# Fused attention and two MLPs: attention in chunks of 11 or 12 blocks instead of 12 and 9, score heads dealt out evenly, x rows at another offset

## The chip, the cores and the metric

The kernel runs on one core of one Trainium2 chip. The metric is the device time of one execution in microseconds. A core has TensorE (PE; its weight loads are shown as PEld), VectorE (DVE), ScalarE (ACT), GpSimd (POOL) and SyncE (SP); in this kernel SP and ACT issue the DMA transfers.

## The reference

Attention over 4 batches, 12 heads, 448 rows and 64 columns, with one 12 x 12 matrix that mixes heads before the softmax and one that mixes them after it. Its output, 1792 rows of 768, goes through two MLPs.

```python
scores = scale * np.matmul(q, k.transpose(0, 1, 3, 2))
scores = np.einsum('bhij,hg->bgij', scores, w_pre)
scores = scores - np.max(scores, axis=-1, keepdims=True)
attn = np.exp(scores)
attn = attn / (np.sum(attn, axis=-1, keepdims=True) + 1e-09)
attn = np.einsum('bhij,hg->bgij', attn, w_post)
attn_out = np.matmul(attn, v)
# x = attn_out as 1792 x 768
x = ((x @ w1) * (x @ w2) @ w3) @ w_out        # first MLP, w1 and w2 768x1024
out = np.maximum(x @ w_in, 0.0) ** 2 @ w_out2  # second MLP, d_ff 2048
```

## The kernel before

All operands are float32; most matmuls split an operand into a high and a low part and add three products (`mm3`). The program has three parts on one core: the product of w3 and w_out (`Prod34`, up to some 125 us), attention, and the MLPs (`Moe`), of which the first matmuls are issued while attention ends.

**Chunks and blocks.** The 448 query rows of a batch are cut into four chunks (`CHUNKS`: first row, rows, blocks), 120, 120, 120 and 88 rows. A chunk is cut into blocks of at most 10 rows, 12, 12, 12 and 9 of them, 45 per batch and 180 in all. `first[n]` is the number of the first block of chunk n, n from 0 to 15. A block holds 10 rows times 12 heads, so that one matmul with a 120 x 120 matrix mixes the heads.

**Score heads.** For a chunk and a head, `scores` does two matmuls (high and low part of q) into one of three PSUM buffers `sc`; `evac` copies it on ACT to the tile `s0` or `s1` (even and odd chunks), which keeps a chunk's 12 heads. The chunk after next uses the same tile again.

**A step.** `attention_step(A, d, ev)` issues step d: two blocks, 2d and 2d+1. `regroup` (SP, L378) brings the blocks 2d+4 and 2d+5 from `s` into the layout with heads on partitions (`r`, six buffers). On TensorE follow `premix` (L386), this step's score heads (L364), `tmix` of the blocks of two steps ago (L442), and `pv`, when it is planned. ACT does, in this order, the exponentials (`expo`), the evacuations of score heads, `p_hi`, its share of `p2` and `pv_out`; DVE does `rowmax`, `p_lo`, the reciprocals, `p2`, and the casts of q and k; POOL does a small addition and the low parts of q and k. The lists `ORDER`, `NEEDS` and `LAG` set this. `pv` multiplies a finished chunk by v, in two halves of 48 TensorE instructions; `pv_out` copies the half and stores it to `xd`.

**The plan.** `attention_plan` puts into every step which heads, loads and casts belong to it. It counts in blocks and halves the number (`ev.setdefault(step // 2, ...)`). The 12 heads of chunk n are spread over the block numbers in which chunk n-1 is on its way:

```python
for t, h in spread(first[n - 1] - RG + AT["sc"], first[n] - RG - 1, range(NH)):
    add(t, "scores", n, h)
```

with `RG` = 4 and `AT["sc"]` = 1. Loads of q are issued 6 block numbers ahead of the first of their four heads, the casts 4 ahead; k's six pairs come every 4 block numbers.

**The end of attention.** In step `closed` = (first[15] - RG) // 2 the tiles of the scores are given up and `Moe`'s pool `wp` takes their place. From there `tail_plan` issues, by block number, the loads of the first quarter's x rows (`load_x`), their split into parts (`split_x`, ACT and POOL), and the loads, joins (three DVE operations each) and splits of the first weights. After the last `pv` come the matmuls `e`, `early` ones of the first MLP; then `begin` loads the second quarter's x rows, and `run` goes through all other units of the MLPs. `new_xy` allocates x rows with some spare columns ahead and behind.

Of the kernel before, what the change touches and what calls it, by code (L numbers as in the profile page):

```python
# [17 lines left out]
B, NH, S, D = 4, 12, 448, 64  # L18
DM, FF1, FF2 = 768, 1024, 2048
NT = B * S  # L20
IC = 120
CHUNKS = [(0, 120, 12), (120, 120, 12), (240, 120, 12), (360, 88, 9)]
JC, JP = 4, 112
TB = 448
HT = 896
# [10 lines left out]
def fused_kernel(ctx, tc, q, k, v, w_pre, w_post, w1, w2, w3t, wo, win, wo2, eye, out):  # L36
# [3 lines left out]
    def pool(stack, name, side="left", space=None):  # L40
        kw = {"space": space} if space is not None else {}
        return stack.enter_context(tc.tile_pool(name=name, bufs=1, side=side, reuse_waits="tile", **kw))
# [5 lines left out]
    def f32(ap):  # L48
        return ap.bitcast(F)
# [179 lines left out]
    for n in range(16):  # L229
        _, ic, nr = CHUNKS[n % 4]  # L230
        o = 0
# [4 lines left out]
    first = {}  # L236
# [4 lines left out]
    RG = 4  # L241

    class Attention:
# [84 lines left out]
        def load_q(self, n, g4):  # L328
            b, c = divmod(n, 4)
            i0, ic, _ = CHUNKS[c]  # L330
            o = 12 * i0 + 4 * g4 * ic
            raw = self.ka.tile([128, 4 * IC], F, tag="qraw", name=f"qraw{n}_{g4}", bufs=2)
            nc.sync.dma_start(raw[:, : 4 * ic], q[b, :, o : o + 4 * ic])
            self.qraw[n, g4] = raw[:, : 4 * ic]

        def high_q(self, n, g4):
            th = self.ka.tile([128, 4 * IC], R, tag="qh", name=f"qh{n}_{g4}", bufs=3)
            th = self.qh[n, g4] = th[:, : 4 * CHUNKS[n % 4][1]]
            if n:
                nc.vector.tensor_copy(th, self.qraw[n, g4])  # L340
            else:
                nc.scalar.activation(th, self.qraw[n, g4], AF.Copy)

        def low_q(self, n, g4):
            tl = self.ka.tile([128, 4 * IC], R, tag="ql", name=f"ql{n}_{g4}", bufs=3)
            tl = self.ql[n, g4] = tl[:, : 4 * CHUNKS[n % 4][1]]
            nc.gpsimd.tensor_tensor(tl, self.qraw.pop((n, g4)), f32(self.qh[n, g4]), ALU.subtract)
# [5 lines left out]
        def scores(self, n, h):  # L353
            b, c = divmod(n, 4)
            ic = CHUNKS[c][1]
            assert ("k", b, h // 2) in self.done
            if h == 0:
                self.st[n] = (self.ka if n % 2 == 0 else self.kc).tile(
                    [IC, NH, S], F, tag=f"s{n % 2}", name=f"s{n}"
                )  # L360
            sc = self.ps.tile([IC, S], F, tag="sc", name=f"sc{n}_{h}", bufs=3)
            g4, hh = divmod(h, 4)
# [6 lines left out]
        def evac(self, n, h):  # L369
            ic = CHUNKS[n % 4][1]  # L370
            nc.scalar.activation(self.st[n][:ic, h], self.sc.pop((n, h))[:ic], AF.Copy)  # L371
            self.done.add(("s", n, h))
# [75 lines left out]
        def p2_evac(self, g, eng):  # L448
            n, r, nr, o, cnt = blocks[g]
            if n not in self.p2:  # L450
                self.p2[n] = self.kb.tile([JP, JC, NH, IC], F, tag="p2", name=f"p2{n}", bufs=2)
            d = self.p2[n][:, :, :, o : o + cnt].rearrange("p j g i -> p (j g) i")
# [40 lines left out]
            eng = nc.sync if n < 15 else nc.scalar  # L493
            eng.dma_start(xd[n // 4, :, 3 * y : 3 * y + 3, o : o + ic], u[:, :, :ic])

    def spread(lo, hi, items):
        return [(lo + i * (hi - lo) // len(items), x) for i, x in enumerate(items)]


    AT = {"sc": 1, "lq": 6, "hq": 4, "pv": 5, "k": -11, "ks": 4, "v": -6}  # L500


    TAIL = {"w": 5, "ws": 2, "w8": 13, "n": 4, "x": -1, "xs": 2, "xn": 4, "xt": 2, "h": 7, "hn": 1}

# [7 lines left out]
    def attention_plan():  # L512
        ev = {}

        def add(step, kind, *a):
            ev.setdefault(step // 2, {}).setdefault(kind, []).append(a)

        for n in range(16):
            b = n // 4
            if n:  # L520
                for t, h in spread(first[n - 1] - RG + AT["sc"], first[n] - RG - 1, range(NH)):
                    add(t, "scores", n, h)
                    if h % 4 == 0:
                        add(t - AT["lq"], "load_q", n, h // 4)
                        add(t - AT["hq"], "high_q", n, h // 4)
            for y in range(2):
                add(first[n + 1] + AT["pv"] + (5 if n < 15 else 0) * y, "pv", n, y)
        for b in range(1, B):
            for r in range(NH // 2):
                t = first[4 * b - 2] + AT["k"] + AT["ks"] * r  # L530
                add(t - 3, "load_k", b, r)
                add(t, "high_k", b, r)
        for b in range(B):
            add(first[4 * b] + AT["v"] if b else -10, "load_v", b)
        return ev


# [45 lines left out]
    class Moe:  # L583
# [95 lines left out]
        def new_xy(self, name, t):  # L679
            p = self.ap if t else self.wp  # L680
            out = []

            for e, before, after in (("h", 24, 0), ("l", 16, 24)):
                if t:
                    before = after = 0
                x = p.tile([128, before + 6 * TB + after], R, tag=f"xy{e}{t}", name=f"{name}{e}{t}")
                out.append(x[:, before : before + 6 * TB].rearrange("p (c n) -> p c n", n=TB))
            return tuple(out)
# [113 lines left out]
    with tc.manual_schedule(), ExitStack() as base:  # L802
        const = pool(base, "const")
        sa, sb, s34, stg, sps = ExitStack(), ExitStack(), ExitStack(), ExitStack(), ExitStack()
        ka = pool(sa, "ka")
        P = Prod34(pool(s34, "p34"), pool(stg, "stg", "right"), ka)
        A = Attention(const, ka, None)
        A.setup_load()
        ev = attention_plan()
        step = iter(range(-5, (first[16] + AT["pv"]) // 2 + 2))  # L810

        def prologue(i):
            def at(kind):
                return [x for x, t in enumerate(PRO[kind]) if t == i]

            if i == PRO["pre"]:
                A.setup_pre()
            for kind in ("load_k", "load_q"):
                for x in at(kind):
                    getattr(A, kind)(0, x)  # L820
            for x in at("evac"):
                if PRO["scores"][x] < i:
                    A.evac(0, 2 * x)
                    A.evac(0, 2 * x + 1)
            for kind in ("low_k", "high_k", "split_q"):
                for x in at(kind):
                    getattr(A, kind)(0, x)
            for x in at("scores"):
                for h in (2 * x, 2 * x + 1):
                    A.scores(0, h)  # L830
                    if PRO["evac"][x] == i:
                        A.evac(0, h)
            if i == PRO["post"]:
                A.setup_post()
            if i == 15:
                stg.close()
                A.kc = pool(sb, "kc", "right")
            if i >= 15:
                for _ in range(PRO["steps"][i - 15]):
                    attention_step(A, next(step), ev)  # L840

        with ExitStack() as s8:
            ps8 = pool(s8, "ps8", space=PSUM)

            P.half0(ps8, prologue)
        A.ps = ps = pool(sps, "ps", space=PSUM)
        tags = iter(("tp", "tp", "pv", "sp", "tp", "tp", "pv", "tp"))

        def space(m):
            tag = next(tags)  # L850
            return ps.tile([128, HC], F, tag=tag, name=f"q34_{m}", bufs=1 if tag == "pv" else 2)

        P.half1(space, lambda i: prologue(8 + i))
        s34.close()
        A.kb = pool(sb, "kb", "right")
        closed = (first[15] - RG) // 2
        M, tail = None, {}
        for d in step:
            attention_step(A, d, ev)
            if d == closed:  # L860
                sa.close()
                M = Moe(pool(sa, "wp"))
                tail = M.tail_plan()
                heads = (x for i in range(2) for x in M.early(
                    i, lambda i: ps.tile([128, TB], F, tag="sc", name=f"e{i}", bufs=3)
                ))
            for g in (2 * d, 2 * d + 1):
                for a in tail.pop(g - 2 * closed - 1, []):
                    a()
                for _ in range(TAIL["hn"] if g >= nb + TAIL["h"] else 0):  # L870
                    next(heads, None)
        for u in sorted(tail):
            for a in tail[u]:
                a()
        for _ in heads:
            pass
        sb.close()
        sm = ExitStack()
        M.begin(pool(sm, "ap", "right"))
        sps.close()  # L880
        M.run(pool(sm, "psm", space=PSUM))
        sm.close()
        sa.close()
# [51 lines left out]
```

## Time and profile before

| | us |
|---|---|
| median of three runs | 1378.08 (1377.71 to 1380.04) |
| the profiled execution | 1376.75 |
| its span, first to last instruction | 1374.9 |
| TensorE busy in it | 1322.3 |
| DVE, ACT, POOL busy in it | 920.9, 708.7, 414.7 |

The profile is of one execution. Its times count from the first instruction. A matmul's end is modelled, so the distance between the starts of two matmuls says more than the length of one. The granted clock of TensorE is given as a share of 2.4 GHz; 0.5 is the lower level, 1.2 GHz, and a value between is a mean over a stretch.

### The profile page before, as it was taken

The page shows a single profiled execution, that of the slowest core. Times are in us where ns is not written, and L with a number is a line of the kernel's source. Part 1 is how long each engine was busy: PE and PEld are TensorE (multiplying, and loading weights), DVE is VectorE, ACT ScalarE, POOL GpSimd, SP SyncE. Part 2 cuts the span into 40 slices and gives each one's busy share as a digit, 9 for nine tenths or more (in the row PEclk, how much of TensorE's full clock was granted, in tenths as well). Part 3 has the DMA queues.
Part 4 walks back from the last instruction along what each step waited for, and adds up shares of the span by engine and source line. Part 5 has one row for each costly group of instructions (what it writes and reads, how often), then busy time and mean ns, then how long its engine had stood idle before and what let it go on. Part 6 is the DMA issues. An engine that isn't in the chain of part 4 may idle for free.

```text
span 1374.9 us, 23972 instructions
## 1 busy us (share of the span) xinstructions
PE 1322.3 (96%) x8858; PEld 1149.9 (84%) x8858; DVE 920.9 (67%) x1555; ACT 708.7 (52%) x1529; POOL 414.7 (30%) x432
## 2 busy tenths in 40 slices
PE   5789999999999997899999999999999999999998
PEld 5687767767767775899999999999999999999998
DVE  8975977887887788555217953986555228945972
ACT  4456877777877876343224533443334224533430
POOL 4541432341342113222222322233222222322231
PEclk9889999999999999999999999999999999999999
DMA  7774445545554435433123432355443123432441
GB/s 213 224 237 139 157 157 171 188 147 179 166 186 148 140 101 161 140 113 113 55 66 104 126 127 81 112 183 178 126 116 96 54 81 103 131 116 81 126 146 58
DMA packets 95513, 183.76 MB, mean 134 GB/s; under 512 B 20581, under 2 KB 62053, under 8 KB 94949
## 3 DMA queue, kind: packets, MB, share of 16 engines
q1 hardware_dynamic: 89861, 178.82, 41.5%
q10 hardware_dynamic: 5536, 3.42, 0.8%
q8 instruction: 70, 1.15, 0.3%
q14 instruction: 46, 0.38, 0.1%
HBM read 129.52 MB, written 14.16 MB: 104 GB/s over the span
## 4 chain that ended last, share of the span: by engine, by line
PE 82%; DVE 5%; ACT 4%; issue 4%; DMA 2%; POOL 1%; SPq 0%; ACTq 0%; DVEq 0%; POOLq 0%
PE l L55 50%; PE y L55 8%; PE sp L386 7%; PE tp L442 6%; PE pv L483 5%; PE sc L364 4%; ACT p L400 1%; PE q L55 1%; DVE f L94 1%; DVE f L96 1%; DMA r<-s 1%; DVE f L98 1%; ACT ph L425 1%; ACT s L371 1%; DVE p L457 1%
## 5 line engine op out<-in xcount | busy, mean ns | idle before, releaser
L116 POOL TENSOR_TENSOR wl<-f,wh 128x384 fp32r<-128x384 f32 (+1 forms) x176 | 195.9, 1117 | 498.2 <-ACT wh L112 483.1
L94 DVE TENSOR_SCALAR f<-y 128x384 int32<-128x384 int32 (+2 forms) x209 | 154.3, 738 | 88.1 <-POOL wl L116 81.3
L386 PE MATMUL sp<-r,kpre 120*120 120x448 f32 x360 | 157.0, 558 | 2.6 <-DMA r<-s 1.4
L400 ACT ACTIVATE p<-sp,nm 120x448 f32<-120x448 f32 x180 | 113.2, 636 | 74.8 <-DVE nm L392 73.1
L392 DVE TENSOR_REDUCE nm<-sp 120x1 f32<-120x448 f32 x180 | 108.4, 620 | 62.5 <-PE sp L386 56.0
L98 DVE SCALAR_TENSOR_TENSOR f<-raw,f 128x384 int32<-128x384 int32 (+2 forms) x209 | 139.6, 668 | 6.2
L96 DVE SCALAR_TENSOR_TENSOR f<-y,f 128x384 int32<-128x384 int32 (+2 forms) x209 | 135.9, 650 | 6.2
L112 ACT ACTIVATE wh<-f 128x384 fp32r<-128x384 f32 (+1 forms) x176 | 96.6, 549 | 83.8 <-DVE f L98 83.2
L55 PE MATMUL l<-blh,wh 128*128 128x448 f32 x384 | 139.4, 363 | 0.0
L55 PE MATMUL l<-bhh,wh 128*128 128x448 f32 x384 | 139.2, 362 | 0.0
L55 PE MATMUL l<-bhh,wl 128*128 128x448 f32 x384 | 138.3, 360 | 0.0
L442 PEld LDWEIGHTS <-ph 120*128 120x128 f16 (+1 forms) x1440 | 108.5, 99 | 30.0 <-issue 29.9
L442 PE MATMUL tp<-kwh,ph 120*128 120x120 f16 x720 | 122.6, 220 | 4.8 <-DVE p L457 4.4
L432 DVE SCALAR_TENSOR_TENSOR pl<-p,sm,ph 120x448 f16<-120x448 f32 x180 | 124.5, 733 | 0.0
L82 ACT ACTIVATE y<-raw 128x384 f32<-128x384 f32 (+2 forms) x209 | 120.6, 577 | 6.4 <-DMA raw<-w3t 3.3
L442 PE MATMUL tp<-kwl,ph 120*128 120x120 f16 x720 | 121.7, 219 | 0.0
L442 PE MATMUL tp<-kwh,pl 120*128 120x120 f16 x720 | 121.7, 219 | 0.0
L425 ACT ACTIVATE ph<-p,sm 120x448 f16<-120x448 f32 x180 | 112.0, 678 | 17.6 <-DVE sm L420 14.7
L415 POOL TENSOR_SCALAR sm<-sm 120x2 f32<-120x2 f32 (+3 forms) x94 | 31.3, 333 | 297.2 <-ACT p L400 283.9
L364 PE MATMUL sc<-kt,qh 128*120 128x448 f32 (+1 forms) x192 | 98.3, 512 | 12.9 <-ACT s L371 9.2
L457 DVE TENSOR_SCALAR p<-tp,iv 112x480 f32<-112x480 f32 (+1 forms) x135 | 91.1, 703 | 9.7 <-PE tp L442 9.3
L371 ACT ACTIVATE s<-sc 120x448 f32<-120x448 f32 (+1 forms) x192 | 92.4, 550 | 8.4 <-PE sc L364 6.1
(122 smaller groups left out, 3139.7 us busy)
## 6 DMA issues: line engine op xcount, KB each, us to landing
r<-s SPq DMA_DIRECT2D x172, 210.0 KB
raw<-w SPq DMA_DIRECT2D x64, 384.0 KB
raw<-win SPq DMA_DIRECT2D x64, 384.0 KB
raw<-wo SPq DMA_DIRECT2D x48, 512.0 KB
kraw<-k SPq DMA_DIRECT2D x24, 448.0 KB
qraw<-q SPq DMA_DIRECT2D x36, 240.0 KB
raw<-w3t SPq DMA_DIRECT2D x15, 512.0 KB
raw<-wo SPq DMA_DIRECT2D x16, 384.0 KB
```

What stands on the lines that cost most here:

```text
L55: nc.tensor.matmul(acc, w, x, start=(first and i == 0 and j == 0), stop=(last and i == n - 1 and j == 2))
L82: nc.scalar.activation(y, self.raw[i][:, :, 1].bitcast(F), AF.Copy, scale=2.0**-112)
L94: nc.vector.tensor_scalar(fi, yi, 3, 0x7FFFFFFF, ALU.logical_shift_left, ALU.bitwise_and)
L96: nc.vector.scalar_tensor_tensor(fi, yi, -0x80000000, fi, ALU.bitwise_and, ALU.bitwise_or)
L98: nc.vector.scalar_tensor_tensor(fi, raw[:, :, 0], 29, fi, ALU.logical_shift_right, ALU.bitwise_or)
L116: nc.gpsimd.tensor_tensor(self.out[i][1], self.ft.pop(i), f32(self.out[i][0]), ALU.subtract)
L364: nc.tensor.matmul(sc[:ic], t[:, hh * ic : hh * ic + ic], self.kt[b, h // 2][:, h % 2], start=(i == 0), stop=(i == 1))
L386: nc.tensor.matmul(t[:kk], self.kpre[:kk, :kk], self.rt.pop(g)[:kk], start=True, stop=True)
L400: nc.scalar.activation(p[:kk], self.sp.pop(g)[:kk], AF.Exp, bias=self.nm.pop(g)[:kk], accum_out=self.sm[g // 2][:kk, g % 2 : g % 2 + 1],)
L425: nc.scalar.activation(self.phl[g % NP][0][:kk, :S], self.pt[g][:kk], AF.Copy, scale=self.sm[g // 2][:kk, g % 2 : g % 2 + 1])
L432: nc.vector.scalar_tensor_tensor(l, self.pt.pop(g)[:kk], self.sm[g // 2][:kk, g % 2 : g % 2 + 1], h, ALU.mult, ALU.subtract)
L442: nc.tensor.matmul(t[:, j, :, :cnt], p[:kk, j * JP : j * JP + 128], w[:kk, :, :cnt], start=(i == 0), stop=(i == 2))
```

## The change

The chunks have 110, 110, 110 and 118 rows, in 11, 11, 11 and 12 blocks; the number of blocks, 45 per batch, and their sizes (43 of 10 rows and 2 of 9) stay, and `IC`, the length of tiles that hold a chunk's rows, is 118. The plan counts in steps. The heads of chunk n go from the step after the last regroup of chunk n-2 (whose tile they take) to the step before the first regroup of chunk n, evenly. Loads of q are 3 steps ahead, their casts 2; k's pairs come 3 to 2 steps, one step after their load. In `new_xy` the first quarter's tiles (the halves' first x rows, t = 0) have 16 and 0 spare columns ahead and 0 and 48 behind, where they had 24 and 16 ahead and 0 and 24 behind.

```diff
-IC = 120
-CHUNKS = [(0, 120, 12), (120, 120, 12), (240, 120, 12), (360, 88, 9)]
+IC = 118
+CHUNKS = [(0, 110, 11), (110, 110, 11), (220, 110, 11), (330, 118, 12)]
...
         def add(step, kind, *a):
-            ev.setdefault(step // 2, {}).setdefault(kind, []).append(a)
-
+            ev.setdefault(step, {}).setdefault(kind, []).append(a)
+
+        lo = {n: (first[n - 1] - 1 - RG) // 2 + 1 for n in range(1, 16)}
         for n in range(16):
             b = n // 4
             if n:
-                for t, h in spread(first[n - 1] - RG + AT["sc"], first[n] - RG - 1, range(NH)):
+                hi = (first[n] - RG) // 2
+                for h in range(NH):
+                    t = lo[n] + h * (hi - lo[n]) // NH
                     add(t, "scores", n, h)
                     if h % 4 == 0:
-                        add(t - AT["lq"], "load_q", n, h // 4)
-                        add(t - AT["hq"], "high_q", n, h // 4)
+                        add(t - 3, "load_q", n, h // 4)
+                        add(t - 2, "high_q", n, h // 4)
             for y in range(2):
-                add(first[n + 1] + AT["pv"] + (5 if n < 15 else 0) * y, "pv", n, y)
+                add((first[n + 1] + 5 + (5 if n < 15 else 0) * y) // 2, "pv", n, y)
         for b in range(1, B):
             for r in range(NH // 2):
-                t = first[4 * b - 2] + AT["k"] + AT["ks"] * r
-                add(t - 3, "load_k", b, r)
+                t = lo[4 * b] - 6 + 3 * r // 2
+                add(t - 1, "load_k", b, r)
                 add(t, "high_k", b, r)
         for b in range(B):
-            add(first[4 * b] + AT["v"] if b else -10, "load_v", b)
+            add((first[4 * b] - 6) // 2 if b else -5, "load_v", b)
...
-            for e, before, after in (("h", 24, 0), ("l", 16, 24)):
+            for e, before, after in (("h", 16, 0), ("l", 0, 48)):
                 if t:
                     before = after = 0
```

## Rows read from the trace of the kernel before

**Rows 1.** The page: TensorE's busy time, and its busy tenths in 40 slices.

```profile
PE 1322.3 (96%) x8858; PEld 1149.9 (84%) x8858; DVE 920.9 (67%) x1555; ACT 708.7 (52%) x1529; POOL 414.7 (30%) x432
...
PE 5789999999999997899999999999999999999998
```

**Rows 2.** Stretches: from:to and length, engines' busy time (instructions), clock, DMA share, GB/s.

```profile
261.92:264.78 2.86, 2.86 (x31) 2.00 (x29) 1.69 (x3) 1.13 (x3) 0.00 (x0) 1.00 0.36 125
...
271.73:275.43 3.70, 3.70 (x35) 2.55 (x33) 2.74 (x5) 1.96 (x6) 0.39 (x1) 1.00 0.82 284
275.43:279.49 4.06, 4.06 (x39) 2.81 (x35) 3.65 (x8) 4.06 (x11) 2.53 (x3) 1.00 0.19 54
255.56:261.92 6.36, 6.36 (x85) 5.06 (x81) 5.87 (x12) 5.73 (x13) 2.74 (x4) 1.00 0.82 281
348.37:354.08 5.71, 5.71 (x84) 4.47 (x80) 5.05 (x11) 5.09 (x14) 1.53 (x3) 1.00 0.74 228
264.78:271.73 6.95, 6.95 (x86) 5.18 (x82) 6.78 (x13) 6.08 (x15) 5.18 (x6) 1.00 0.28 90
133.91:507.36 373.45, 363.89 (x3817) 269.31 (x3813) 304.04 (x573) 299.23 (x705) 116.24 (x160) 1.00 0.49 162
507.36:553.99 46.63, 39.02 (x487) 30.17 (x485) 38.42 (x66) 28.28 (x63) 13.21 (x14) 0.93 0.50 147
186.21:196.59 10.38, 7.69 (x88) 5.70 (x84) 7.26 (x13) 7.42 (x17) 6.29 (x7) 1.00 0.62 212
292.35:301.79 9.44, 7.69 (x88) 5.62 (x85) 7.72 (x14) 6.76 (x16) 5.78 (x6) 1.00 0.46 149
305.87:311.87 6.00, 4.70 (x41) 3.26 (x37) 4.46 (x7) 5.95 (x14) 3.62 (x4) 1.00 0.28 96
402.52:414.56 12.04, 9.07 (x89) 7.20 (x85) 6.71 (x13) 7.45 (x17) 5.98 (x7) 0.86 0.52 183
196.59:200.69 4.10, 4.10 (x36) 3.02 (x35) 2.60 (x5) 2.35 (x7) 0.32 (x1) 1.00 0.00 0
...
515.85:520.01 4.16, 3.02 (x30) 2.02 (x29) 2.90 (x6) 2.63 (x7) 0.40 (x1) 1.00 0.83 269
520.01:525.17 5.16, 4.71 (x28) 3.00 (x29) 3.54 (x7) 3.41 (x8) 2.12 (x2) 0.67 0.68 187
525.17:528.42 3.25, 2.98 (x32) 1.96 (x28) 2.86 (x6) 3.13 (x7) 0.57 (x1) 1.00 0.99 297
528.42:535.07 6.65, 5.72 (x76) 4.45 (x76) 6.56 (x8) 3.71 (x9) 3.91 (x4) 1.00 0.61 191
535.07:541.07 6.00, 3.06 (x30) 2.06 (x29) 4.19 (x10) 4.10 (x10) 1.95 (x2) 1.00 0.00 0
```

The engines in these rows are PE, PEld, DVE, ACT and POOL, in this order.

**Rows 3.** TensorE's waits from 133.91 to 507.36 us: total us, times, longest.

```profile
PE sc L364 <- ACT s L371: 8.5, 4, 3.0
...
PE sp L386 <- DMA r<-s: 0.2, 1, 0.2
```

**Rows 4.** Order of time, TensorE, step 17: start us, length, instruction, wait before it.

```profile
192.10 0.47 PE L364 MATMUL sc<-kt,qh 128*120 128x448 f32 x1 [2.68 <-ACT s L371]
```

**Rows 5.** Instructions on `sc`, 133.91 to 507.36 us: count, min/median/max ns, shapes.

```profile
L364 PE MATMUL sc<-kt,qh x166: 361/370/720, 135.1 to 503.0; 128*120 128x448 f32 x118, 128*88 128x448 f32 x48
```

**Rows 6.** TensorE's waits from 507.36 to 600 us.

```profile
PE l L55 <- ACT x0h L702: 2.2, 1, 2.2
PE l L55 <- DVE x0l L704: 1.2, 1, 1.2
PE sp L386 <- DMA r<-s: 1.1, 1, 1.1
```

**Rows 7.** Order of time, SP's DMA issues, 499 to 565 us (start us, length).

```profile
512.92 0.40 SPq L494 DMA_DIRECT2D xd<-xs  x1
...
548.29 13.19 SPq L70 DMA_DIRECT2D raw<-w  x6
561.54 1.27 SPq L696 DMA_DIRECT2D x0l<-xd  x2
```

More of the change, by code (lines that the diff above doesn't have):

```diff
@@ L494, in pv_out @@
             eng.dma_start(xd[n // 4, :, 3 * y : 3 * y + 3, o : o + ic], u[:, :, :ic])
-    def spread(lo, hi, items):
-        return [(lo + i * (hi - lo) // len(items), x) for i, x in enumerate(items)]
-    AT = {"sc": 1, "lq": 6, "hq": 4, "pv": 5, "k": -11, "ks": 4, "v": -6}
     TAIL = {"w": 5, "ws": 2, "w8": 13, "n": 4, "x": -1, "xs": 2, "xn": 4, "xt": 2, "h": 7, "hn": 1}
@@ L809, in fused_kernel @@
         ev = attention_plan()
-        step = iter(range(-5, (first[16] + AT["pv"]) // 2 + 2))
+        step = iter(range(-5, (first[16] + 5) // 2 + 2))
         def prologue(i):
```

## The prediction

> **What bounds the kernel now.** I read the page first, then one row per attention step, then TensorE's waits. The page puts TensorE at 96% of the span, and its slices stand at 9 except in the first 100 us and in two slices near 520 to 580 us [rows 1]. So time can come back only where TensorE waits. The change touches attention: an attention step mixes two of the 180 blocks, and I cut the stretch at the first premix matmul of every step. Step 5 starts at 133.91 us, step 83 at 507.36 us, and e (the first MoE matmuls) at 553.99 us [rows 2].
>
> Inside the stretch the lengths are regular [rows 2]. A step without score heads and without a `pv` half takes 2.86 us, with two heads 3.70, with three 4.06; with two heads and a 120-row `pv` half 6.36, with an 88-row half 5.71. TensorE is busy for all of each: it bounds these steps, and a step is a sum of parts: 2.86, plus 0.41 per head ((3.70 - 2.86) / 2 = 0.42, (4.06 - 2.86) / 3 = 0.40), plus 2.66 per 120-row half (6.36 - 3.70) or 2.01 per 88-row half. That is 0.0203 us per row of a half: (2.66 - 2.01) / 32.
>
> Four steps break the rule, and they are the four in which four heads are issued [rows 2]: 10.38 us (step 17), 9.44 (39), 6.00 (41) and 12.04 (62), where 2.86 + 4 x 0.41 = 4.50, with a half 7.16, is expected. They are 3.22, 2.28, 1.50 and 4.88 too long, 11.88 together. The waits say why: four waits of the score matmul for ACT's evacuation of scores, 8.5 us, are nearly all that TensorE's records show as waiting there [rows 3]. `sc` has three buffers, so the fourth head of a step needs the first one evacuated, and on ACT the evacuations stand behind the step's two exponentials. In step 17 the fourth head starts at 192.10, after 2.68 us of waiting for that evacuation [rows 4]. In step 62 the granted clock averages 0.86: part of it ran at the lower level of 1.2 GHz, so it is 1.66 us longer than step 17, which has the same content at 1.00.
>
> Why four: chunk 3 of a batch has 9 blocks, and the 12 heads of the next chunk are spread over 7 block numbers while it runs. For chunk 4: 33 + h x 7 // 12, halved, gives steps 16 to 19 with 2, 4, 3, 3 heads. Chunk 12 repeats this at 61 to 64; chunk 8 gives 4, 3, 4, 1 at 39 to 42.
>
> **The change part by part.**
>
> *Heads.* With 11, 11, 11, 12 blocks the chunks start at blocks 0, 11, 22, 33, 45, 56, 67, 78, 90, ... The new rule gives 3, 2, 3, 2, 2 heads in five steps (chunk 8: two in each of six). I wrote out all 16 chunks: no step has four, and no three-head step follows a three-head step. The fourth-head wait has nothing left to arise from: -11.88. What is late next there? Three buffers take three heads; three-head steps run at 4.06, and the half in 264.78:271.73 made one 6.95, 0.2 above the sum [rows 2].
>
> *The whole stretch.* Before, steps 5 to 82 hold 78 steps, 166 heads [rows 5] and 27 `pv` halves (21 of 120 rows, 6 of 88): 223.08 + 68.06 + 55.86 + 12.06 = 359.1 us. Measured 373.45: 14.4 more, of which 11.9 are the four steps and 2.5 small excesses. After, chunk 15 begins at block 168 instead of 171, so the last heads are issued in step 81, one step earlier, and steps 5 to 81 hold 77 steps, 165 heads, 21 halves of 110 rows (2.46 each) and 6 of 118 (2.62): 220.22 + 67.65 + 51.66 + 15.72 = 355.3. I keep the 2.5 (border steps without heads followed by three heads occur on both sides): 357.8. Change: **-15.65**. Bounds of the 2.5: 0 to twice that.
>
> *Start.* Fifteen heads instead of 14 are issued before step 5: **+0.4**.
>
> *Loads and casts.* Instructions, bytes and lags of `load_q`, `high_q`, `low_q` stay (3, 2 and 1 steps ahead); only the tiles get 440 or 472 columns for 480 or 352, with the same total. Key loads come one step before their cast, which two of the three batches have now. POOL's two `low_k` come in adjacent steps instead of every second one; that is part of the 2.5's upper bound. SP's order per step is unchanged.
>
> *Operand addresses.* Runs of q, p2 and xs are multiples of 480 or 352 B now, of 440 or 472 B after. No row shows such a run, so I price it by the rows of either length, which lie on one line through the same overhead: 0. The Trainium skill (SBUF — State Buffer, section "Door 1: The DMA port swizzle") says that SBUF lines are of 16 bytes and that each crossing into a new line costs. By it a run of 440 B that starts off such a boundary touches one line more in about 28, an estimate of 3.6% of the halves, 3 us over 32 of them; the sum below would be -9 instead of -12. No row here shows it either way.
>
> *The end.* From 507.36 to 553.99 TensorE no longer leads: five steps have neither head nor half by the plan, and they take 2.86, 4.16, 5.16, 3.25 and 6.00 us (the four longer ones in [rows 2]) because DVE, ACT and POOL carry x rows and weights as well. The changed kernel has one such step more between the last head and e: eight instead of seven. Its price is between 2.86 (TensorE alone) and 6.65 (the longest in that stretch); I take **+5.0**, between the mean of the five, 4.29, and the 6.00 of the last, which it most resembles (it lies among the first weight joins). The `pv` halves: 15.0 and 15.1 have 118 rows instead of 88 and run with nothing beside them, +1.2; 13.1, 14.0 and 14.1 lose 10 rows each, -0.6: **+0.6** (to +1.2). The wait for regrouped rows in 515.85:520.01 stays: the x load and the regroups stand behind the `xd` store that SP issues at 512.92 [rows 6, 7], and the new order has the same halves around the same place.
>
> After e TensorE waits 2.2 and 1.2 us for the second quarter's x rows [rows 6]. Their load (561.54) stands on SP behind six weight loads issued from 548.29 to 561.48 [rows 7], each into a buffer that a DVE join has to free. The tail's plan counts from the step after chunk 14's last regroup, so weights start a step earlier against the last blocks, and e starts later: I take back **-2.5**, bounds 0 and -3.4.
>
> *x rows' offset.* The padded tiles still add up to 64 spare columns, so nothing behind them in `wp` moves by it; the same old tiles lie under them. 0.
>
> Sum: -15.65 + 0.4 + 5.0 + 0.6 - 2.5 = **-12.15**. The profiled execution took 1376.75 us (span 1374.9), so 1364.6; the median of the three runs is 1.33 above it: 1378.08 - 12.15 = **1365.9 us**. Bounds together: -15.65 - 2.5 + 0.4 + 2.86 + 0.6 - 3.4 = -17.7, and -15.65 + 2.5 + 0.4 + 6.65 + 1.2 = -4.9.
>
> **Rivals.**
>
> A, the end eats more: the extra step at 6.65, the halves at +1.2, nothing back, and the small excesses doubled because heads are denser where two chunks follow without an empty step (24 heads in 10 steps, 2.4 per step, against 2.13 over the stretch). For it: DVE is busy 304 and ACT 299 of 373 us [rows 2], and 304 / 357.8 is 85%. Against: per step TensorE has work for 2.86 + 2.4 x 0.41 + 0.4 x 2.46 = 4.8 us there, and DVE averages 304 / 78 = 3.9, ACT 3.8. -4.9: 1373.
>
> B, the change doesn't remove the wait: it comes from ACT being behind and moves to three-head steps. Then 11.88 stay, -0.3: 1378. For it: step 41 waits without any `pv`. Against: 196.59:200.69, three heads right behind a four-head step, takes 4.10 [rows 2].
>
> C, slower: SP's queue. A store of `xd` waits in SP for ACT two steps after its half and holds back the regroups behind it. In step 85 that made TensorE wait 1.1 us for `r` [rows 6]; that step lost 4.16 - 2.86 = 1.30, and the next, at a granted clock of 0.67, 5.16 - 2.86 = 2.30 [rows 2]. Price 3.6 us per event. The new order leaves two steps of 3.70 and 4.06 after some halves (steps 21 and 66, where a three-head step follows). From four events on (4 x 3.6 = 14.4) the kernel is slower, at 1380. Against: before, step 27's half is followed by 3.70, 4.06 and 3.65, and in the whole stretch a single wait for `r` shows, 0.2 us [rows 3].
>
> **How the numbers follow.** Forecast (heads' wait gone, end dearer): 0.70. A: 0.17. B: 0.08. C: 0.05. The forecast's own range is -17.7 to -8, A's centre is -4.9. Leaving out a tenth on either side gives 1360.5 to 1373. A measurement of this kernel tells about 0.2% (2.8 us) from no change. Faster: 0.70, plus nearly all of A, 0.15, is 0.85; same: most of B and the rest of A, 0.09; slower: C and a little of B, 0.06.
>
> **What would show it.** Right: no wait of `sc` for ACT's evacuation above 0.5 us; step 81's end (start of step 82) about 357.8 us after step 5's start; the granted clock at 1.00 through the stretch; start of step 82 to e about 52 us; x waits after e below 3.4. Wrong: waits of `sc` in three-head steps (B); waits of premix for `r` in the stretch (C); DVE or ACT without gaps and premix waiting for the exponentials at borders such as steps 8 to 10 (A); `pv` halves of 110 rows longer than 2.66 us (the addresses).

## The result and the profile after

The changed kernel takes 1365.36 us in the median (1363.70 to 1367.65), the kernel before 1379.06 us (1377.12 to 1382.79) in six runs each on one chip. The ratio is 0.9898, with a 95% interval of 0.9883 to 0.9913. The forecast was 1365.9, so the time is right. Its sum is not: the stretch with heads gave 3.3 us less than forecast, the end cost 4.0 us more, and a gain of 5 us at which the prediction put 0 covers most of both.

The profiled execution took 1365.69 us (span 1363.9), 11.06 less than that of before. On the page after, TensorE's slices stand at 8 and 9 where [rows 1] has 7 and 8 (the sixteenth and seventeenth, some 511 to 580 us), and of these two the granted clock is down to 8 in the sixteenth.

```profile
PE 1318.2 (97%) x8858; PEld 1149.8 (84%) x8858; DVE 920.3 (67%) x1555; ACT 706.4 (52%) x1529; POOL 419.1 (31%) x432
...
PE   5789999999999998999999999999999999999998
...
PEclk9989999999999998999999999999999999999999
```

The same stretches as [rows 2], after the change. First five step shapes: no head, two heads, three heads, two heads with a half of 110 rows, three heads right behind an empty step. Then step 59, the whole stretch (start of step 5 to start of step 82), and from there to e, which is called the end below. The columns are those of [rows 2].

```profile
468.22:471.08 2.86, 2.86 (x30) 2.00 (x29) 2.09 (x4) 1.12 (x3) 0.00 (x0) 1.00 0.66 184
...
406.61:410.25 3.64, 3.64 (x36) 2.57 (x33) 3.23 (x5) 3.64 (x10) 3.01 (x3) 1.00 0.08 23
402.52:406.61 4.09, 4.09 (x36) 2.97 (x35) 3.52 (x8) 2.58 (x8) 2.57 (x3) 1.00 0.26 100
410.25:416.41 6.16, 6.16 (x85) 4.85 (x81) 5.26 (x11) 5.66 (x13) 0.74 (x2) 1.00 0.76 240
471.08:475.60 4.52, 4.31 (x39) 2.89 (x35) 4.44 (x9) 3.75 (x11) 1.58 (x2) 1.00 0.25 70
386.83:391.51 4.68, 3.03 (x31) 2.00 (x29) 2.21 (x5) 1.68 (x5) 1.23 (x1) 1.00 0.70 214
134.57:495.64 361.07, 357.92 (x3786) 266.03 (x3782) 301.31 (x566) 294.28 (x698) 120.40 (x159) 1.00 0.58 165
495.64:551.87 56.23, 46.82 (x514) 35.77 (x512) 43.59 (x75) 32.31 (x72) 14.46 (x16) 0.85 0.54 150
```

TensorE's waits in the stretch, which answer to [rows 3], and the heads, which answer to [rows 5]:

```profile
PE sp L386 <- ACT p L400: 1.7, 1, 1.7
PE sc L364 <- POOL ql L347: 0.7, 3, 0.2
PE tp L442 <- ACT p L455: 0.2, 1, 0.2
```

```profile
L364 PE MATMUL sc<-kt,qh x165: 360/367/720, 135.8 to 491.5; 128*110 128x448 f32 x117, 128*118 128x448 f32 x48
```

No score matmul waits for ACT's evacuation any more (8.5 us in [rows 3]), the clock is 1.00 throughout, and the stretch is 12.38 us shorter. What is behind it is longer: 56.23 us at a mean clock of 0.85, against 46.63 at 0.93 in [rows 2]. TensorE's waits from 495.64 to 600 us, which answer to [rows 6]:

```profile
PE tp L442 <- DVE p L457: 2.3, 2, 1.3
PE sp L386 <- DMA r<-s: 2.0, 1, 2.0
...
PE pv L483 <- DVE p L457: 1.2, 1, 1.2
...
PE l L55 <- DVE x0l L701: 0.7, 1, 0.7
...
PE l L55 <- ACT x0h L699: 0.4, 1, 0.4
```

The balance of the two profiled executions, by the starts of step 5, of the first step behind the last heads, of e, and of the first matmul y, the first MLP's second product, by w3 and w_out (before at 675.97, after at 668.84 us):

| part | before | after | difference | forecast |
|---|---|---|---|---|
| start to step 5 | 133.91 | 134.57 | +0.66 | +0.4 |
| stretch with heads | 373.45 | 361.07 | -12.38 | -15.65 |
| from there to e | 46.63 | 56.23 | +9.60 | +5.6 |
| e to y | 121.98 | 116.96 | -5.02 | -2.5 |
| y to the end | 698.92 | 695.08 | -3.84 | 0 |

The remaining 0.08 us lies outside the spans.

### The profile page after: what moved, and what is told of

It reads as the page before. It is cut to its first block, busy times and chain, and to the rows that moved or that the text cites. A ratio compares the mean times of both kernels' runs of the same rounds, so it can differ in the third digit from the quotient of the medians.

```text
span 1363.9 us, 23983 instructions
## 1 busy us (share of the span) xinstructions
PE 1318.2 (97%) x8858; PEld 1149.8 (84%) x8858; DVE 920.3 (67%) x1555; ACT 706.4 (52%) x1529; POOL 419.1 (31%) x432
## 4 chain that ended last, share of the span: by engine, by line
PE 80%; DVE 6%; issue 5%; ACT 4%; DMA 3%; POOL 1%; SPq 0%; ACTq 0%; DVEq 0%; POOLq 0%
PE l L55 50%; PE y L55 8%; PE sp L386 7%; PE tp L442 5%; PE pv L483 4%; PE sc L364 4%; PE q L55 1%; ACT p L400 1%; DVE f L94 1%; DMA kraw<-k 1%; DVE f L96 1%; DVE f L98 1%; ACT ph L425 1%; POOL ql L347 1%; ACT s L371 1%
## 5 line engine op out<-in xcount | busy, mean ns | idle before, releaser
L364 PE MATMUL sc<-kt,qh 128*110 128x448 f32 (+1 forms) x192 | 97.1, 506 | 4.1 <-DVE kt L325 3.2
L386 PEld LDWEIGHTS sp<-r,kpre 120*120 120x120 f32 x360 | 58.9, 184 | 46.6 <-issue 21.7
L371 ACT ACTIVATE s<-sc 110x448 f32<-110x448 f32 (+1 forms) x192 | 92.4, 552 | 7.3 <-PE sc L364 6.2
```

Of the source, the lines that this page charges most:

```text
L364: nc.tensor.matmul(sc[:ic], t[:, hh * ic : hh * ic + ic], self.kt[b, h // 2][:, h % 2], start=(i == 0), stop=(i == 1))
L386: nc.tensor.matmul(t[:kk], self.kpre[:kk, :kk], self.rt.pop(g)[:kk], start=True, stop=True)
```

## The experiments

Every run also carries the changed kernel's edits unless its diff says otherwise. Times are medians, and ratios are to the kernel before on the same chip, with 95% intervals.

### The offset, and the parts of the change one by one

**e1_old_offset**, the changed kernel with the old spare columns:

```diff
-            for e, before, after in (("h", 16, 0), ("l", 0, 48)):
+            for e, before, after in (("h", 24, 0), ("l", 16, 24)):
```

> The changed kernel with the x rows' spare columns as they were (24 and 16 ahead). Seen in the two traces: in the MLPs a group of 18 matmuls that reads x or y rows takes 3640 ns before and 3600 ns after; 128 such groups would be 5.1 us. Theory O (the offset sets it): 3640 ns again, 5.1 us slower than the changed kernel, ratio to before about 0.9935. Rival P (it is a matter of one execution, or of something else that the chunks changed): 3600 ns, ratio 0.990. The attention stretch (step 5 to the end of step 81) stays at 361 us by both.

Measured: 1372.42 us, 0.9946 [0.9933, 0.9958]: without the offset only about half of the gain is left. From y to the end it takes 698.91 us, as before.

**e2_offset_only**, the kernel before with the same line the other way round.

> The kernel before with only the x rows' new spare columns. Theory O: groups of 18 at 3600 ns, about 5 us faster, ratio 0.996 to 0.997. Rival P: 3640 ns, ratio 1.000. The four waits of the fourth score head, 8.5 us, stay by both, and the stretch (steps 5 to 82) stays at 373 us.

Measured: 1375.49 us, 0.9968 [0.9957, 0.9979]; y to the end 695.07, as after. The four waits stay at 8.5 us. The stretch was expected at 373 us and took 378.02 in the profiled execution, with one wait of 1.8 us for `r` and 10.2 us at half clock (the lower level), where before has 0.2 and 3.4; the edit moves nothing that runs there, and why it took longer was not tried.

The offset's gain shows in single groups of matmuls. Here are two groups of 18 that follow each other in the first MLP of the second 896 rows. The first reads the tiles of t = 0, which the change moves, the second those of t = 1, whose place it leaves alone. The kernel before comes first, then the changed one.

```profile
979.81:983.48 3.68, 3.68 (x19) 3.38 (x18) 3.37 (x7) 0.58 (x1) 0.39 (x1) 1.00 0.39 108
983.48:987.09 3.60, 3.60 (x19) 3.38 (x18) 1.81 (x5) 1.39 (x3) 1.02 (x1) 1.00 0.66 205
```

```profile
971.23:974.83 3.60, 3.60 (x19) 3.38 (x18) 3.30 (x7) 0.58 (x1) 0.39 (x1) 1.00 0.41 109
974.83:978.43 3.60, 3.60 (x19) 3.37 (x18) 1.89 (x5) 1.39 (x3) 1.01 (x1) 1.00 0.69 204
```

The reader is to see the same instructions and the same clock, with only the group at the moved address shorter, by some 0.08 us. There are 64 such groups, which makes 5 us: 48 behind y (3.84 us) and 16 ahead of it.

**e3_deal_only**, the new plan on the old chunks, with the old offset:

```diff
-IC = 118
-CHUNKS = [(0, 110, 11), (110, 110, 11), (220, 110, 11), (330, 118, 12)]
+IC = 120
+CHUNKS = [(0, 120, 12), (120, 120, 12), (240, 120, 12), (360, 88, 9)]
```

> The kernel before with only the new plan: the old chunks of 12, 12, 12, 9 blocks and the old x rows' offset, heads dealt over whole steps (four steps in a row of three heads each at steps 16, 39 and 61, none with four). Theory F (the loss is the fourth head of a step): no wait of the score matmul for ACT's evacuation above 0.5 us, the stretch of steps 5 to 82 at 360 to 364 us instead of 373, the end as before; 10 to 12 us faster, ratio 0.991 to 0.993. Rival D (ACT is behind in dense places, and the chunks' evenness is what helps): waits of 1 to 3 us in each of the three rows of three-head steps, stretch 367 to 373, ratio 0.996 to 1.000.

Measured: 1369.05 us, 0.9926 [0.9913, 0.9938]. Dealing alone removes the wait of `sc`; the old chunks keep the short end (501.78 to 546.56). The stretch is 367.17 us, above the 360 to 364 that were expected, and a wait that the kernel before hardly has is its largest:

```profile
PE sp L386 <- DMA r<-s: 3.0, 2, 2.5
PE sc L364 <- POOL ql L347: 0.7, 3, 0.2
```

**e4_chunks_only**, the old plan (`spread`, `AT`, `step // 2`) on the new chunks and the new offset.

> The changed kernel with the old plan in block numbers: chunks of 11, 11, 11, 12 and the new offset. By the old rule no step then has four heads either, but three-head steps follow each other. Theory F: stretch within 2 us of the changed kernel's 361 (the key loads come every second step again, so the 1.8 us lost at step 59 may go), time within 2 us of it, ratio 0.989 to 0.991. Rival D': the even dealing in whole steps is what matters: waits in the pairs of three-head steps, 4 us or more slower than the changed kernel, ratio 0.993 or above.

Measured: 1365.57 us, 0.9900 [0.9887, 0.9914], with a stretch of 359.77 and an end of 57.96 us. The chunks alone do as much as chunks and dealing: with 11 blocks the old rule spreads the heads over 9 block numbers instead of 7, and no step gets four. Step 59 takes 2.86 us here, with k's loads spaced as before, against 4.68 in the changed kernel.

### Why the end grew

**e5_short_last**, chunks whose last one is short again, so that the last heads come a step later and seven steps without heads are left instead of eight:

```diff
-IC = 118
-CHUNKS = [(0, 110, 11), (110, 110, 11), (220, 110, 11), (330, 118, 12)]
+IC = 120
+CHUNKS = [(0, 120, 12), (120, 120, 12), (240, 110, 11), (350, 98, 10)]
```

> The changed kernel with chunks of 12, 12, 11 and 10 blocks (120, 120, 110 and 98 rows). Chunk 15 then begins at block 170, the last heads are issued in step 82 as in the kernel before, and seven steps without heads follow instead of eight; three steps in a row have three heads at 16 to 19 and 61 to 64. Theory T (the end costs some 10 us more in the changed kernel because a step moved into it, where TensorE idles and its clock falls): start of step 83 to e 45 to 48 us instead of 56, half clock there 7 us at most instead of 17, stretch of steps 5 to 82 at 363 to 367; 3 to 6 us faster than the changed kernel, ratio to before 0.985 to 0.988. Rival (the new plan or the 118-row halves, and not the count of steps, make the end dear): end at 53 us or more, no faster than the changed kernel, ratio 0.990 or above.

Measured: 1378.95 us, 0.9987 [0.9974, 0.9999]. The end was as expected, 47.93 us at a clock of 0.93, but the stretch took 377.81, and the gain was lost there:

```profile
133.46:511.27 377.81, 365.54 (x3817) 269.71 (x3813) 302.85 (x573) 298.07 (x706) 118.87 (x160) 0.99 0.52 159
511.27:559.20 47.93, 39.01 (x486) 30.47 (x484) 37.13 (x66) 28.50 (x63) 12.44 (x14) 0.93 0.51 151
```

```profile
PE sp L386 <- DMA r<-s: 10.1, 3, 4.3
```

The three waits for regrouped rows are in steps 22, 45 and 67, three steps behind the loads of v in steps 19, 42 and 64. (So are those of e3, in steps 22 and 67, and the 1.8 us of e2, in step 22.) SP's order of issues around the first, and TensorE's premix that waits for the first of the four regroups:

```profile
204.17 0.76 SPq L470 DMA_DIRECT2D v<-v  x1
205.02 3.84 SPq L378 DMA_DIRECT2D r<-s  x4
```

```profile
214.79 1.73 PE L386 MATMUL sp<-r,kpre 108*108 108x448 f32 x4 [2.83 <-DMA r<-s]
```

The regroup issued at 205.02, right behind 1344 KB of v, was waited for until 214.79, 9.8 us later. The trace's DMA packets say what went first: a packet of v has 12288 bytes, one of a regroup 1792, and all 71 packets that started from 207 to 210 us have 12288.

### k's loads

**e6_k_earlier**: k's loads two steps ahead of their casts instead of one.

```diff
-                add(t - 1, "load_k", b, r)
+                add(t - 2, "load_k", b, r)
```

> The changed kernel with each load of k two steps ahead of its cast instead of one. In the changed kernel step 59 took 4.68 us instead of 2.86, with premix waiting 1.65 us for an exponential, and the chain of waits runs over a load of k there. Theory K (the cast of k on DVE waits for its load and holds up the row maxima behind it): step 59 at 2.9 to 3.2, no wait above 0.5 us in the stretch, stretch 358.5 to 359.5 instead of 361.1, 2 us faster than the changed kernel. Rival (DVE or ACT is full there, whatever the load does): step 59 stays above 4 us, stretch 361.

Measured: 1367.16 us, 0.9897 [0.9880, 0.9915], no gain. In the changed kernel's step 59 DVE waits for k's rows (386 to 397 us); with the edit it waits for q's instead (386 to 400 us). First the changed kernel, then e6:

```profile
DVE kt L316 <- DMA kraw<-k: 2.5, 1, 2.5
```

```profile
DVE qh L340 <- DMA qraw<-q: 2.1, 1, 2.1
```

Step 59 fell from 4.68 to 3.99 us, but the stretch rose from 361.07 to 362.95. So the late load does delay the step (e4, where k's loads are spaced otherwise, has no delay there), but moving it one step ahead moves the lateness to another load.

### Which of the two parts must move

**e7_h_only** and **e8_l_only**, spare columns with the high part's rows at their old place and the low part's 64 bytes behind their place in the changed kernel (e7), and the high part's as in the changed kernel and the low part's 64 bytes ahead of the old place (e8):

```diff
-            for e, before, after in (("h", 16, 0), ("l", 0, 48)):
+            for e, before, after in (("h", 24, 0), ("l", 8, 32)):   # e7
+            for e, before, after in (("h", 16, 0), ("l", 8, 40)):   # e8
```

> The changed kernel with the high part of the first quarter's rows 32 bytes further on (where it was before, a multiple of 64 bytes) and the low part's rows at 32 bytes past a multiple of 64, as the second quarter has both. The groups of 18 matmuls on the first quarter's rows took 3677 ns before and 3600 after; the low part is read by one of three matmuls, the high part by two. If the place of the high part alone decides: 3677 again. If each matmul pays for its own rows: 3650. If it is the low part: 3600.

> The changed kernel with the low part of the first quarter's rows at a multiple of 64 bytes and the high part as changed (32 bytes past one). If the high part alone decides: 3600 ns per group of 18. If each matmul pays for its own rows: about 3626. If it is the low part: 3677. If neither multiple matters but the distance between the two parts: any value, and not the complement of the run before.

Measured in one run each: 1370.44 and 1368.52 us, y to the end 697.31 and 697.01, between 695.08 and 698.9. The two groups as above, e7 and then e8:

```profile
974.56:978.21 3.64, 3.64 (x19) 3.38 (x18) 3.34 (x7) 0.58 (x1) 0.39 (x1) 1.00 0.38 105
978.21:981.81 3.60, 3.60 (x19) 3.38 (x18) 1.84 (x5) 1.39 (x3) 1.01 (x1) 1.00 0.69 203
```

```profile
972.85:976.49 3.64, 3.64 (x19) 3.38 (x18) 3.33 (x7) 0.58 (x1) 0.39 (x1) 1.00 0.40 115
976.49:980.09 3.60, 3.60 (x19) 3.38 (x18) 1.84 (x5) 1.39 (x3) 1.01 (x1) 1.00 0.63 198
```

In both runs a group takes 0.04 us longer than in the changed kernel, and 0.04 less than before. If each matmul paid for the rows that it reads, 3.650 (e7) and 3.626 (e8) were expected: e7 comes near, e8 does not.

### The load of v

Three kernels with v's load cut into four pieces of 336 KB, 13 to 10 steps earlier; then one with the pieces around the old place.

```diff
-            add((first[4 * b] - 6) // 2 if b else -5, "load_v", b)
+            for j in range(JC):
+                add((first[4 * b] - 6) // 2 - 13 + j if b else -5, "load_v", b, j)   # e9, e10, e11
+                add((first[4 * b] - 6) // 2 - 3 + j if b else -5, "load_v", b, j)    # e12
```

**e9_short_last_v**, on the chunks of e5:

> Chunks of 12, 12, 11 and 10 blocks (as in e5_short_last), and the load of v (1.38 MB in one piece) cut into four of 344 KB that are issued 13 to 10 steps earlier, one a step. Theory V: in e5_short_last the waits of TensorE for regroups (2.83 us in step 22, 3.00 in step 45, 4.26 in step 67, of 10.1 us in all) come from the v load that stands in the same queue just ahead of them. Then no wait of over 0.5 us for `r` is left in the stretch from step 5 on, the stretch takes 361 to 365 us instead of 377.8, the steps behind the last heads 46 to 48 us with 7 us at half clock as in e5_short_last, and the time is about 1361 us, ratio to the kernel before 0.984 to 0.988. Rival (the queue's instructions are held up on SP by the store of x rows, or ScalarE's evacuations come late of themselves): the waits of 2 to 4 us in steps 22, 45 and 67 stay and the time is about 1377 us, ratio 0.997 to 1.0.

Measured: 1361.51 us, 0.9865 [0.9850, 0.9879]. The stretch and the end, its waits, and the same four regroups, now behind a load of q:

```profile
133.44:498.92 365.48, 361.84 (x3816) 267.97 (x3812) 302.88 (x573) 297.64 (x706) 118.98 (x160) 1.00 0.54 165
498.92:545.58 46.66, 37.73 (x486) 29.19 (x484) 37.52 (x66) 28.38 (x63) 12.44 (x14) 0.93 0.52 151
```

```profile
PE sp L386 <- ACT p L400: 1.7, 1, 1.7
PE sc L364 <- POOL ql L347: 1.3, 4, 0.4
```

```profile
204.57 0.73 SPq L333 DMA_DIRECT2D qraw<-q  x1
205.39 3.44 SPq L378 DMA_DIRECT2D r<-s  x4
```

All three waits for `r` are gone. The stretch is 12.3 us shorter than e5's (half a microsecond above the upper end of what was expected), which settles where e5's went.

**e10_changed_v**, on the changed kernel:

> The changed kernel with the same edit of the load of v alone. Its stretch has no wait for `r` of note, so theory V expects little: stretch 359 to 361.5 us (before the edit 361.1), steps behind the last heads 55 to 58 us, time 1363 to 1366 us, ratio 0.988 to 0.990. If four loads cost more on the queue than one, or hold up the loads of k and q behind them, the stretch is 363 or more and the time 1367 or more.

Measured: 1368.93 us, 0.9917 [0.9900, 0.9933], 0.0019 above the changed kernel's ratio, with intervals that overlap. In the profiled execution the stretch took 366.60 us, 5.5 more, so there the edit wasn't neutral. Its step 33 ran with the DMA engines 0.88 busy, waited for `r`, and then fell to half clock; the pieces of v had come between the loads of k and q, ahead of regroups that were due:

```profile
265.74:275.65 9.91, 9.31 (x81) 6.65 (x81) 7.14 (x12) 6.48 (x15) 6.20 (x7) 0.66 0.88 232
```

```profile
PE sp L386 <- DMA r<-s: 3.0, 3, 2.1
```

```profile
256.26 1.40 SPq L310 DMA_DIRECT2D kraw<-k  x1
257.71 0.42 SPq L471 DMA_DIRECT2D v<-v  x1
258.23 1.71 SPq L378 DMA_DIRECT2D r<-s  x2
```

**e11_old_chunks_v**, the old chunks with the new plan and offset:

> The changed kernel's plan and offset on the old chunks of 12, 12, 12 and 9 blocks, with the load of v cut and earlier as in e9_short_last_v. e3_deal_only had the same plan on the same chunks with the old offset and the whole load: stretch 367.2 us with 3.0 us of waits for `r`, end 44.8. Theory V: the waits go, the stretch takes 362 to 365 us, the end stays at 44 to 46 us, the offset gives its 5 us, and the time is about 1360 us, ratio 0.984 to 0.987. Rival (the waits aren't the load's): stretch 366 to 368 us, time about 1364 us, ratio 0.988 to 0.990 by the offset alone.

Measured: 1358.96 us, 0.9853 [0.9835, 0.9871], the fastest of all. Its stretch and end:

```profile
133.39:496.55 363.16, 361.55 (x3817) 268.04 (x3813) 302.96 (x573) 297.48 (x705) 120.81 (x160) 1.00 0.51 166
496.55:542.67 46.12, 39.04 (x486) 29.70 (x484) 37.45 (x66) 28.34 (x63) 12.89 (x14) 0.93 0.51 148
```

**e12_v_cut_only**, the same with the pieces around the old place:

> e11_old_chunks_v (the changed kernel's plan and offset on the old chunks, ratio 0.9853) with the four loads of v around the old place, from 3 steps before it to the step itself, instead of 13 to 10 steps earlier: behind the loads of k (steps 30 to 37), no longer among them. It tells apart what helped in e11: the pieces or the earlier place. Theory P (pieces: a regroup queued behind 1.38 MB lands late, one behind 344 KB doesn't): no wait of over 0.5 us for `r` in the stretch from step 5 to step 83, the stretch 362.5 to 364 us, time 1357 to 1360 us, ratio 0.984 to 0.987. Rival E (the place: what is loaded there, in one piece or in four, meets regroups that are due soon): waits for `r` of 1.5 to 2.5 us come back near steps 22, 45 or 67, stretch 365 to 367 us, time about 1362 us, ratio 0.987 to 0.989.

Measured: 1360.23 us, 0.9866 [0.9849, 0.9882], stretch 363.03 us, and no wait for `r` in it. On the old chunks the pieces are enough; the earlier place adds nothing that these runs can tell. Why it did harm on the new chunks (e10) and none on the old ones (e11) was not tried apart.

## Why the prediction was right or wrong

**The four-head waits: right.** They are gone in after, e3 and e4, and stay at 8.5 us in e2, which keeps the old plan and chunks. Three-head steps take 4.09; rivals B and C did not come in the changed kernel. (C's wait for `r` did in e3 and e5, by v's load and not by the store of `xd`.) Each of two edits suffices, which the prediction did not see: it put the cause in the 9-block chunk and the rule together, and either one mended removes it.

**The stretch: -12.38 instead of -15.65.** The rule for a step held (2.86, 3.64, 4.09). The failed term is the "2.5 small excesses": they are 361.07 - 355.3 = 5.8. Step 59 took 4.68 instead of 2.86, because DVE waited 2.5 us for k's load; step 60 was 0.55 late behind it; and each of the four other three-head steps without a half right behind an empty step took 4.44 to 4.52 instead of 4.06: 4.0 together, and the rest in steps of a few tenths. Bounds of "0 to twice that" were a little too narrow.

**Operand addresses: 0 holds.** Steps with two heads and a half took 5.71 us with 88 rows and 6.36 with 120 [rows 2]. The line through them gives 6.16 for 110 rows, and 6.16 is what such a step took. By a single half, 6.16 - 3.64 = 2.52 us against the forecast 2.46, 32 halves would cost 1.9 us at most. By the rule of the Trainium skill (SBUF — State Buffer, section "Door 1: The DMA port swizzle") the price was an estimate of 3 us; the rows show less.

**The end: +9.60 instead of +5.6.** The step more was priced well: steps 82 to 88 take 528.22 - 495.64 = 32.58 us, before 83 to 88 took 535.07 - 507.36 = 27.71, so +4.87. What failed is the part from the start of step 89 on, which the prediction left as it was but for the halves' rows. (The 6.00 us that the prediction reads for step 89 end inside a wait of TensorE of 3.50 us, 538.13 to 541.63, so step 89 is not cut off here.) First the changed kernel's end, the last row from step 89 to e, then that part in the kernel before:

```profile
504.56:509.62 5.06, 3.03 (x31) 2.03 (x29) 3.30 (x7) 2.72 (x7) 0.40 (x1) 1.00 0.74 227
509.62:514.10 4.48, 4.48 (x29) 3.09 (x29) 2.70 (x5) 3.09 (x8) 2.23 (x2) 0.63 0.60 145
...
522.34:528.22 5.88, 3.14 (x33) 1.95 (x29) 5.00 (x9) 3.90 (x10) 2.32 (x3) 0.97 0.33 110
528.22:534.22 6.00, 6.00 (x32) 3.89 (x34) 5.30 (x10) 3.64 (x9) 1.16 (x2) 0.50 0.66 191
528.22:551.87 23.65, 19.47 (x220) 16.22 (x220) 18.55 (x33) 10.46 (x23) 6.18 (x7) 0.72 0.52 137
```

```profile
535.07:553.99 18.92, 14.09 (x223) 12.32 (x221) 15.68 (x30) 10.23 (x22) 5.49 (x5) 0.91 0.39 109
```

This part is 4.73 longer. TensorE is busy for 5.38 longer in it, at a mean clock of 0.72 instead of 0.91, and idle for 0.65 less; some 1 us of the busy time is forecast, the halves' rows. In this end the clock fell around the ends of steps 84 and 88 (at 510.8 and 527.9), in which TensorE was busy for 3.03 of 5.06 and 3.14 of 5.88 us; around step 59 (3.03 of 4.68) it did not. In all, 17.1 us between step 82 and e ran at half clock, 6.8 before. How the loss splits between clock and waits differs between runs (e1 has 10.2 us at half clock and an end just as long, 57.1). What holds in every profile is the count of steps: with eight behind the last heads (after, e1, e4, e6, e7, e8, e10) the end takes 54.6 to 58.1 us, with seven (before, e2, e3, e5, e9, e11, e12) 44.8 to 47.9. So an end with the eighth step is about 10 us longer, and not only by the 5 of that step's own length. All seven kernels that have it also have the changed kernel's chunks, with 118 rows in the last two halves instead of 88 or 98; by the prediction's price per row that is some 1 us of the 10, and it was not tried apart.

**x rows behind e: right in direction.** The waits of 2.2 and 1.2 us are 0.4 and 0.7, -2.3 of the forecast -2.5. The other 2.7 of this part were not forecast: 16 groups by the offset (e1 against after 1.16, e2 against before 1.12), and about 1.6 that go with 3.4 us at half clock, which are gone (from e to 600 us the mean clock was 0.96 before and is 1.00 after).

**x rows' offset: wrong.** "0" was the step that failed most. It looked only at what lies behind the padded tiles, not at where a tile's own rows start. Without its 5.0 us the profiled execution would have taken 1370.7; e1, which is just that, took 1371.67, and 1372.4 in the median. That is near rival A's 1373. Two of A's terms came, the small excesses more than doubled and a dearer end. But the excesses sit mostly behind k's load and at borders with an empty step, and the end's extra time comes with the lower clock from step 89 on. So the mechanism of the stretch was right, and that the time came within 0.6 us of the forecast was luck: +3.3 and +4.0 us of errors met -6.4 us in terms that were not seen or too small.

## What to carry to other kernels

Heads that pile up in one step are mended by dealing them out; the chunks can stay as they are. With v's load in pieces the old chunks were the fastest here (e11, e12), since the last chunk's size sets how many steps at the end have too little for TensorE. Ahead of small transfers that are due, cut a large load on the same queue into pieces, and look again at what the pieces meet. When a tile moves, compare the same matmuls at the old and the new address.

## What was not expected of the hardware

A matmul's time depended on where its moving operands start. In the compiled program's allocation the tiles of t = 0 held their rows, within a partition, from 25856 (high) and 36672 (low) bytes on before, both multiples of 64, and from 25824 and 36576 after, both 32 more than a multiple. The tiles of t = 1, at 164832 and 175584, are of the latter kind and had 3.60 us all along. e7 (high at 25856, low at 36640) and e8 (25824 and 36608) fill the other two cases. With both parts at a multiple of 64, high alone, low alone and neither, 18 matmuls of 448 columns took 3.68, 3.64, 3.64 and 3.60 us. Read so, each part adds the same 0.04, though two of three matmuls read the high part and one the low.

That reading has a rival which these runs leave standing, and which e8's expectation names: the distance between the two parts. It is 10816 bytes before, 10784 in both e7 and e8, and 10752 after and in the tiles of t = 1, so it orders the times just as well. Whether the multiples or the distance count, whether 64 is the step, and whether the place of the weights counts too, was not tried. That the offset alone makes the 5 us is shown either way, by e1 and e2.
